# Chunk 1's down projection by Strassen's scheme over token halves, interleaved with two output projections

## The chip, the cores and the metric

One core of one Trainium2 chip runs the whole kernel. The metric is the device time of one execution in microseconds, lower is better. "Clock" is the mean granted TensorE clock as a share of full speed.

The engines are called as in the profile: PE is TensorE (matmuls), PEld its weight loads, DVE is VectorE, ACT is ScalarE, POOL is GpSimd, SP issues DMAs.

## The reference, cut to what matters

```python
# x: 1 x 2048 x 1024, w_down: 3584 x 1024, all bfloat16
x = A_x
h = x + attention(layernorm(x), A_wqkv) @ A_wo        # windowed attention, 32 heads
n = layernorm(h)
out = h + ((n @ B_w_gate) * (n @ B_w_up)) @ B_w_down  # no activation between
```

The kernel takes the tokens in four chunks of 512. For chunks 2 and 3 together ("pair stage" and "last stage") it already uses Strassen's scheme, that is seven products in place of eight, for the gate, up and down projections. Chunks 0 and 1 are plain.

## The kernel before: the parts that the change touches

```python
def ffn2(c, hf, hT, hs, between={}):                  # half of the output columns
    acc = [psum.tile([128, 512], F32, tag="mm", ...) for t in range(4)]
    for b in range(4):
        for j in range(7):
            f = b * 7 + j
            for t in range(4):
                nc.tensor.matmul(acc[t][:], lhsT=hT[f][:, bass.ts(t, 128)],
                                 rhs=wts["wd", c, hf, b][:, j, :],
                                 start=(f == 0), stop=(f == NF - 1))
            ...
    for t in range(4):
        ffn2_store(c, t, hf, acc[t], hs)              # DVE adds, SP stores
# ...
hT = ffn1(1, lnT2)                                    # first projection of chunk 1
scale_gu.rows(); scale_d.rows()
bg.finish(atts[2])
l2, hs2 = wo_ln2(2)                                   # output projection 2, layer norm
scale_gu.total(); scale_d.total()
# ... loads chunk 3's rows
ffn2(1, 0, hT, hs)                                    # down projection of chunk 1, half a
bg.finish(atts[3])                                    # ends with POOL issuing the oT load
l3, hs3 = wo_ln2(3)                                   # output projection 3, layer norm
activation_sums(l2, l3)
# ...
ffn2(1, 1, hT, hs, {0: first_sums})                   # half b
# ... pair stage, then the last stage:
conv_down(down["b12"])
scale_h.rows()
add_homes(t1v, Fv("b12"), Fv("b11"), ALU.subtract)
conv_down(down["b21"])                                # on DVE
```

`bg` is a helper that puts the attention of a chunk on DVE piece by piece between other work. In the traces each engine runs its instructions in the order of the program text: in the changed kernel POOL goes from the oT issue (483.05 us) to four conversions (486.77 to 514.74) and then to two subtractions (525.21 and 534.18).

## Time and profile before

| | before |
|---|---|
| time, median of 4 | 785.36 us (784.77 to 785.96) |
| PE busy | 774.1 us of 785.8 |
| first projection of chunk 1 ends | 449.5 us |
| output projections 2, 3 and down projection 1 | 449.5 to 525.9 |
| pair stage | 525.9 to 695.1 |
| last stage | 695.1 to 785.8 |

PE is the bound nearly everywhere. The lines that show it stand in the prediction below. One more row matters: the clock, part 2 of the page, in tenths of full speed for 40 slices of 20 us. It never leaves 9; a digit is the mean of its slice, so the 3.4 us of half clock near the start (0.57 from 9.3 to 12.7 us), which the prediction names, do not show in it.

```profile
PEclk9999999999999999999999999999999999999999
```

### The profile page before, as it was taken

Reading aid. Unit: us, or ns where it says so; the run is one execution under the profiler, and the core shown is the slowest. Engines: PE = TensorE matmul, PEld = TensorE weight load, DVE = VectorE, ACT = ScalarE, POOL = GpSimd, SP = SyncE. Lnnn points to the kernel's source line nnn. Section 1 sums busy time; section 2 is a strip of 40 time slices with the busy share of each in tenths; the row PEclk is TensorE's granted clock in tenths of the full one; section 3 lists DMA queues with packets and bytes.
Section 4 is the critical chain, followed back from the end, with each engine's and each line's share of the span. In section 5 each row is a group of like instructions: output and inputs, shape, how many; then the busy total and the mean of one; then the engine's idle time right before and its main releaser. Section 6 shows DMA issues by size and latency. Waiting matters only on the chain.

```text
span 785.8 us, 10287 instructions
## 1 busy us (share of the span) xinstructions
PE 774.1 (99%) x3670; PEld 359.2 (46%) x3732; DVE 583.6 (74%) x727; ACT 402.9 (51%) x919; POOL 150.9 (19%) x160
## 2 busy tenths in 40 slices
PE   8999999999999999999999999999999999999998
PEld 6544444444444444444444444444444444444444
DVE  5619999999899998999979971733443444579862
ACT  3626534323476652965656610116677777749240
POOL 0000000010000200002000020058678687600000
PEclk9999999999999999999999999999999999999999
DMA  7999594895965878867556489433332423730001
GB/s 248 269 197 243 150 286 98 244 311 127 337 203 170 260 243 234 277 197 264 198 161 208 139 202 328 101 100 102 107 90 72 108 62 100 257 118 28 1 27 54
DMA packets 183683, 135.94 MB, mean 173 GB/s; under 512 B 79056, under 2 KB 176464, under 8 KB 181584
## 3 DMA queue, kind: packets, MB, share of 16 engines
q1 hardware_dynamic: 180048, 113.27, 51.0%
q0 software_dynamic: 3584, 22.02, 8.1%
q8 instruction: 29, 0.48, 0.3%
q14 instruction: 22, 0.18, 0.1%
HBM read 106.95 MB, written 22.02 MB: 164 GB/s over the span
## 4 chain that ended last, share of the span: by engine, by line
PE 74%; DVE 20%; issue 2%; SPq 1%; DMA 1%; ACT 0%; DVEq 0%
PE pu L386 12%; PE acc L605 12%; PE pg L386 12%; PE pz L658 6%; PE py L658 6%; PE px L658 6%; PE wo L507 5%; DVE prod L426 4%; PE ps L386 3%; PE pv L658 3%; PE dx L837 3%; PE dy L837 3%; DVE pv L469 2%; DVE prod L428 2%; SPq L223 1%
## 5 line engine op out<-in xcount | busy, mean ns | idle before, releaser
L386 PE MATMUL ps<-lnT,w_qkv 128*128 128x512 bf16 x721 | 159.0, 379 | 0.8
L386 PEld LDWEIGHTS <-w_qkv 128*128 128x128 bf16 x736 | 71.9, 98 | 86.0 <-issue 0.3
L386 PE MATMUL pu<-lnT,w_wu 128*128 128x512 bf16 x438 | 105.1, 379 | 0.6
L386 PE MATMUL pg<-lnT,w_wg 128*128 128x512 bf16 x440 | 105.1, 379 | 0.4
L605 PE MATMUL acc<-w_wd,gs 128*128 128x512 bf16 x438 | 96.7, 379 | 0.5
L300 ACT CAST sg<-ps 128x512 bf16<-128x512 f32 x96 | 54.8, 590 | 52.7 <-PE ps L386 48.9
L469 DVE TENSOR_TENSOR pv<-vD,at 128x4096 bf16<-128x4096 bf16 x32 | 72.5, 2286 | 0.3
L426 DVE TENSOR_TENSOR prod<-qD,kD 128x4096 bf16<-128x4096 bf16 x32 | 72.4, 2284 | 0.1
L658 PEld LDWEIGHTS <-sw 128*128 128x128 f16 x448 | 43.8, 98 | 52.9
L386 PEld LDWEIGHTS <-w_wg 128*128 128x128 bf16 x448 | 43.8, 98 | 52.8
L605 PEld LDWEIGHTS <-gs 128*128 128x128 bf16 x448 | 43.8, 98 | 52.9
L386 PEld LDWEIGHTS <-w_wu 128*128 128x128 bf16 x448 | 43.8, 98 | 52.9
L179 ACT ACTIVATE rs<-mv,eps 128x1 f32<-128x1 f32 x32 | 9.5, 297 | 101.2 <-DVE mv L176 98.2
L585 ACT CAST us<-pu 128x512 bf16<-128x512 f32 x56 | 33.1, 591 | 50.4 <-PE pu L386 49.3
L507 PE MATMUL wo<-w_wo,oT 128*128 128x512 bf16 x251 | 55.6, 379 | 0.3
L658 PE MATMUL px<-lnT,ws 128*128 128x512 bf16 x211 | 52.6, 379 | 0.6
L658 PEld LDWEIGHTS <-ws 128*128 128x128 f16 x336 | 32.9, 98 | 39.6
L481 POOL DMA_DIRECT2D od<-oD x4 | 2.2, 544 | 249.3 <-DVE oD L479 162.5
L637 POOL TENSOR_TENSOR sw<-ws 128x512 f16<-128x512 f16 x28 | 32.3, 1154 | 87.8 <-PE acc L605 47.2
L580 ACT CAST gs<-pg 128x512 bf16<-128x512 f32 x56 | 33.1, 591 | 12.8 <-PE pg L386 8.7
L507 PEld LDWEIGHTS <-oT 128*128 128x128 bf16 x256 | 25.0, 98 | 30.2
L428 DVE TENSOR_TENSOR prod<-prod 128x4096 bf16<-128x4096 bf16 x16 | 36.6, 2288 | 0.3
(244 smaller groups left out, 1196.6 us busy)
## 6 DMA issues: line engine op xcount, KB each, us to landing
w_wg<-in_B_w_gate_dram SPq DMA_DIRECT2D x14, 1024.0 KB, 6.7
w_wu<-in_B_w_up_dram SPq DMA_DIRECT2D x14, 1024.0 KB, 5.6
w_wd<-in_B_w_down_dram SPq DMA_DIRECT2D x16, 896.0 KB, 8.1
w_wo<-in_A_wo_dram SPq DMA_DIRECT2D x8, 1024.0 KB, 7.4
w_pair<-in_B_w_gate_dram SPq DMA_DIRECT2D x14, 512.0 KB, 4.0
w_pair<-in_B_w_up_dram SPq DMA_DIRECT2D x14, 512.0 KB, 5.3
w_qkv<-in_A_wqkv_dram SPq DMA_DIRECT2D x5, 1024.0 KB, 9.7
kd<-sg SPq DMA_DIRECT2D x32, 144.0 KB, 2.8
```

Of the source, the lines that this page charges most:

```text
L300: nc.scalar.copy(sg[:, HB:HB + TC], ps[:])
L386: nc.tensor.matmul(ps[:], lhsT=wt[:, ko, bass.ts(j, 128)], rhs=rhs[:, ko, :], start=(ko == 0), stop=(ko == KO - 1))
L426: nc.vector.tensor_tensor(prod[:, j], qD[:], kD[:, :, o:o + SUB], ALU.mult)
L428: nc.vector.tensor_tensor(prod[:, :, 0:16], prod[:, :, 0:16], prod[:, :, 16:32], ALU.add)
L469: nc.vector.tensor_tensor(pv[:, j], vD[:, :, o:o + SUB], at[:, w, None, :].to_broadcast((128, DH, SUB)), ALU.mult)
L507: nc.tensor.matmul(ps[:], lhsT=oTs[c][:, kk, t, :], rhs=wts["wo", c, hf][:, kk, :], start=(kk == 0), stop=(kk == KO - 1))
L580: nc.scalar.copy(gs[:], pg[:])
L585: nc.scalar.copy(us[:], pu[:])
L605: nc.tensor.matmul(acc[t][:], lhsT=hT[f][:, bass.ts(t, 128)], rhs=wts["wd", c, hf, b][:, j, :], start=(f == 0), stop=(f == NF - 1))
L637: nc.gpsimd.tensor_tensor(sw[:, i, 0], a21, a22, ALU.add)
L658: nc.tensor.matmul(ps[:], lhsT=lhs[:, ko, :], rhs=rhs[:, ko, :], start=(fresh and ko == 0), stop=(ko == 3), skip_group_check=not fresh)
L837: nc.tensor.matmul(ps[:, bass.ds(lo, n)], lhsT=lhs[k][:, bass.ts(q, 128)], rhs=rhs[k][:, bass.ds(lo, n)], start=(fresh and k == 0), stop=( ...
```

## The change

Its intent: save 28 of 224 matmuls in chunk 1's down projection. Seven products P1 to P7 over token halves (2 row tiles each), contraction halves (14 blocks each) and output halves replace eight. The weights have to be converted from bf16 to scaled f16 and then combined (T1, T2, T3 and so on), and the activations likewise (S1, S2, S3). b11 to b22 are the quarters of the weights: the first digit is the half of the contraction, the second the half of the output columns. Each quarter lies in two tiles of 128x3584; `kx` and `vx` hold the two halves of T1 and later of P6's operand (T2 is written over b11), and `prodx`, `ox` and `lx` are the names that the profile gives to other tiles of b12 and b22. This preparation is spread over DVE, ACT and POOL, and the products are interleaved with output projections 2 and 3 so that there is time for it. The core of the diff, other lines cut:

```diff
-    hT = ffn1(1, lnT2)
-    l2, hs2 = wo_ln2(2)
-    ffn2(1, 0, hT, hs)
-    l3, hs3 = wo_ln2(3)
-    ffn2(1, 1, hT, hs, {0: first_sums})
+    def first_blocks():
+        ...
+        conv_down(dn["11"], nc.gpsimd)                      # POOL, 2 x 128x3584
+    hT = ffn1(1, lnT2, {0: scale_d.rows, 2: scale_d.total, 6: first_blocks})
+    conv_down(dn["21"], nc.scalar)
+    bg.finish(atts[2])
+    for q in range(2):
+        dprod(ex[q], q, E1["11"], fcells(dn["11"]), True)   # P1
+    def second_blocks():
+        bg.finish(atts[3])                                  # POOL: oT load of chunk 3
+        ...
+        conv_down(dn["12"] + dn["22"], nc.gpsimd)           # POOL, 4 x 128x3584
+    wo_adds(2, {1: scales, 3: second_blocks, 4: ..., 6: lambda: t1_half(0), 7: lambda: t1_half(1)})
+    for k in range(NP):
+        nc.vector.tensor_tensor(S1[k], EF["21"][k], EF["22"][k], ALU.add)
+    sub(dn["12"], dn["22"], dn["12"], nc.gpsimd)            # POOL, 2 x 128x3584
+    ...                                                     # P2, P3
+    wo_adds(3, {0: lambda: s2(0, 7), ..., 2: lambda: t2_half(0), ...})
+    for k in range(NP):
+        nc.gpsimd.tensor_tensor(EF["12"][k], EF["12"][k], EF["11"][k], ALU.subtract)
+    sub([dn["kx"], dn["vx"]], dn["21"], dn["11"])
+    for t in (2, 3):
+        ln_stats(2, t)
+    for t in range(4):
+        ln_stats(3, t)
+        ln_rows(2, t, l2)
+    for q in range(2):
+        dprod(ey[q], q, EF["11"], fcells(dn["11"]), False)  # P4
+        nc.scalar.copy(ex[q][:], ey[q][:])
+    ...                                                     # P5, P6, P7
-    for i in range(11):                                     # warm-up matmuls
+    for i in range(13):
-    conv_down(down["b21"])                                  # last stage
+    conv_down(down["b21"], nc.gpsimd)
```

## The prediction

> **What bounds the kernel now.** I read the page first (busy shares, chain that ended last, costliest groups), then the table of windows over the stretch that the change touches, then the timeline there. The page:
>
> ```profile
> PE 774.1 (99%) x3670; PEld 359.2 (46%) x3732; DVE 583.6 (74%) x727; ACT 402.9 (51%) x919; POOL 150.9 (19%) x160
> ...
> L605 PE MATMUL acc<-w_wd,gs 128*128 128x512 bf16 x438 | 96.7, 379 | 0.5
> ...
> L637 POOL TENSOR_TENSOR sw<-ws 128x512 f16<-128x512 f16 x28 | 32.3, 1154 | 87.8 <-PE acc L605 47.2
> ```
>
> TensorE is busy 774 of 786 us, and the down projections of chunks 0 and 1 (the second row) found it idle for 0.5 us in all: there is nothing to gain but matmuls, and any new wait is paid in full. The windows are: first projection of chunk 1 (353 to 449), then output projection 2, down projection 1a, output projection 3, down projection 1b (449 to 526):
>
> ```profile
> 353.00:449.00 96.00, 95.53 (x437) 43.55 (x445) 89.56 (x83) 60.94 (x110) 4.63 (x6) 1.00 0.58 189
> 449.00:526.00 77.00, 76.63 (x352) 34.90 (x357) 40.03 (x75) 5.62 (x19) 13.13 (x13) 1.00 0.70 190
> ```
>
> Columns after the width: busy PE, PE loads, DVE, ACT, POOL, then the granted clock. In the second window PE is full, DVE has 37 us free, ACT 71, POOL 64. So there is room for the new work; the question is its order. The timeline gives the order, and the row that I lean on most is the POOL one:
>
> ```profile
> 449.52 13.98 PE L507 MATMUL wo<-w_wo,oT 128*128 128x512 bf16 x63
> ...
> 463.80 3.71 POOL L484 DMA_DIRECT2D oT<-od  x4 [9.97 <-PE l1psgu L544]
> ```
>
> The transpose of chunk 3's attention into oT is issued by POOL, which stood idle for 10 us until output projection 2 had ended (463.5): there is one oT buffer, and those matmuls read it. The issue takes POOL 3.7 us. Before, nothing stood behind it.
>
> [...] The trace shows half clock only at the start (0.57 from 9.3 to 12.7 us), after idle; the rest says nothing. [...]
>
> **The change, part by part.**
>
> *Removed.* Down projection 1 is 2 x 4 x 28 = 224 matmuls of 128x512. Seven products over half the tokens (2 row tiles) and half the contraction (14 blocks) are 7 x 2 x 14 = 196. A matmul starts every 0.216 us (output projection 2: 64 in 13.98 us of the row above), so 28 x 0.216 = **6.05 us** go. One weight load of output projection fewer is off the path. In the last stage one conversion (2 x 1.15 us) leaves DVE; PE waited there 1.0 and 0.3 us on DVE's dn_t2 halves, so about **1 us** goes.
>
> *Added to PE.* One matmul for the new scale (0.2 us). Two more warm-up matmuls lie where PE waits for the first data anyway: 0.
>
> *Added elsewhere, hidden.* In the first projection ACT gets 28 absolute sums (0.62 + 0.19 us), 0.8 of each 3.46 us group; it was idle 1.1 us there, so it fits. POOL converts two blocks there, having 91 us free.
>
> *Added on the path.* PE's new order is P1 (28 matmuls, 6.05 us), output projection 2, P2, P3, output projection 3, P4, P5, P6, P7. By the order of instructions on each engine and what each waits for, two products come too early for their operands.
>
> P3 multiplies S1 by T1 = b12 - b11. POOL converts b12, in two blocks, but behind the issue of oT for chunk 3. With E the end of output projection 2: issue ends E+0.3+3.7 = E+4.0; [...]then DVE, in its queue: the second half of T1 (1.95, the 128x3584 subtraction is 2.01 in the last stage), the 14 additions for S1 (14 x 0.20; half of the 0.41 of a 512 addition) 2.8, and the result of P2 that frees the accumulator 0.75: E+15.7. PE has only P2 until then, E+6.1. **Wait: 9.6 us.**
>
> P5 starts from a copy of P4's accumulator on ACT, and that copy stands behind chunk 2's normalised rows, which need DVE. With G the end of output projection 3, DVE does: last addition 0.7, two subtractions 3.9, six layer-norm statistics of 1.44 each (two of 0.68 less overlap, plus 0.21 and gaps: 492.20 to 493.64 in the timeline) 8.6, four small ones 0.6: G+13.8. Then ACT, one row of 128x1024 (1.06) and the copy (0.57), with handovers 2: G+15.8. PE has P4, until G+6.3. **Wait: 9.5 us**, and DVE comes to G about 1.7 us late, as in that stretch it is given S2, T2 and statistics beside the additions: **11.2 us.**
>
> [...]the clock should drop in each[...]: **about 4 us** for both. P6, P7 and the start of the pair products are then late enough that their operands are there.
>
> Sum: 785.4 - 6.05 - 1 + 0.2 + 9.6 + 11.2 + 4 = 803.4; I take **803 us**.
>
> **The rivals.**
>
> (a) *All hidden.* If conversions and statistics keep up, only the arithmetic remains: 785.4 - 6.05 - 1 + 0.2 = 778.5. For it: the free time in the window, and that such a schedule will have been tuned with a profile at hand, with warm-up counts and engines chosen finely. Against it: [...]the two queues above are in the program. Nothing can make the change faster by over 2%, since that is 15.7 us.
>
> (b) [...]POOL's two subtractions of 128x3584 (7 x 1.154 = 8 us each, estimate) and 14 small ones now lie beside DVE's two-input work. If each blocks the other, both waits grow by up to a subtraction: 810 to 825. [...]no row of the trace speaks for or against.
>
> (c) *One wait only.* If the conversions took 1 us, P3's wait would be 5.4; if the statistics of chunk 3 were done during output projection 3, P5's wait would be about 2. Either alone gives 790 to 796. At 8 us per conversion P3's wait would be 19 and the sum 813.
>
> (d) *Weight loads.* The blocks of 0.9 MB land in 8.1 us and are issued well ahead; the queue's share was 0.70. The loads for b12 and b22 wait for attention 3's buffers, which are free at 453. Hidden, I think; one landing late would add 1 to 3 us at P2 or P3.
>
> **Range and chances.** Each of the two waits rests on queue order[...] and on durations of which one (conversion on POOL) is not measured: plus or minus 6. The clock is plus or minus 3,[...] a better overlap than I see only downward. Low 789 (one wait halved and no clock loss), high 817[...]. Slower by over 2% begins at 801.1, just under the middle, and I give the tuner's eye some weight: slower 0.53, same 0.46, faster 0.01.
>
> **What would show it.** Right: an idle time of PE of 7 to 13 us ahead of P3, released by DVE's T1 or result, with POOL going straight from the oT issue into its conversions; a second of 8 to 14 us ahead of P5, released by ACT's copy, which itself follows the row activations; granted clock of half in the window after each; matmuls in the two down projections down by 28. Wrong: PE busy without a gap from 449 to the pair stage (then rival a, near 779);[...] DVE or POOL operations much longer where they lie side by side than alone (rival b).

## The result, and the profile after

The changed kernel takes 879.89 us (median of 4, 879.69 to 880.63). Ratios here are the mean time of one kernel's fast runs over that of the other's of the same rounds, so not quite the ratio of the medians: 1.1205, with a 95% interval of 1.1186 to 1.1225. The forecast was 803 with 817 as the upper end: the direction was right, the size was far off.

First the rows that answer to those shown before: part 1 of the page, the clock row, and the two windows with the same columns.

```profile
PE 780.9 (89%) x3707; PEld 356.4 (41%) x3707; DVE 677.3 (77%) x799; ACT 450.6 (51%) x1019; POOL 255.6 (29%) x184
...
PEclk9999999999999999999978755979999999998999
```

```profile
353.00:449.00 96.00, 95.64 (x444) 43.17 (x442) 89.54 (x80) 69.12 (x150) 26.43 (x7) 1.00 0.59 192
449.00:526.00 77.00, 29.03 (x114) 11.78 (x113) 56.81 (x46) 29.36 (x50) 44.28 (x11) 0.67 0.29 93
```

In the stretch from 449 to 526 us PE falls from 76.63 us to 29.03, and its clock to 0.67. The view of PE's waits says what it waited for (waiter, releaser: us in total, times, longest):

```profile
PE ex L782 <- DVE h L787: 55.5, 1, 55.5
PE ex L782 <- ACT ex L925: 13.9, 1, 13.9
PE ex L782 <- DVE gs L597: 8.6, 2, 6.8
PE dy L550 <- DVE rowbh L546: 7.2, 1, 7.2
PE wo L827 <- DVE h L829: 2.6, 2, 1.4
PE ex L782 <- POOL w_dn L763: 2.5, 1, 2.5
```

The 55.5 us are ahead of P3, the 13.9 ahead of P5: the two waits of the prediction. The 8.6 and 2.5 stand inside P1, the 7.2 in the last stage; those I had not foreseen. By stage, from the starts of PE's rows in the two timelines:

| stretch | before | after | difference |
|---|---|---|---|
| start to the end of chunk 1's first projection | 449.5 | 447.0 | -2.6 |
| output projections 2, 3 and down projection 1 | 76.4 | 163.4 | +87.0 |
| pair stage | 169.2 | 169.2 | 0 |
| last stage | 90.7 | 98.6 | +7.9 |

The profile before is of an execution of 787.53 us, 2.2 us over its median of 785.36; so the differences add up to 92.3 us and not to the 94.5 of the medians, and part of the -2.6 belongs to that one execution (see the warm-up matmuls below).

Now the timeline of POOL and of DVE around the long wait (start, us, engine, line, operation; in brackets the idle time before). E, the end of output projection 2, is 482.7 here.

```profile
483.05 3.70 POOL L490 DMA_DIRECT2D oT<-od  x4 [14.81 <-PE wo L827]
486.77 9.34 POOL L763 TENSOR_SCALAR w_dn<-w_dn,sbd 128x3584 f16<-128x3584 bf16 x1
496.11 9.32 POOL L763 TENSOR_SCALAR prodx<-prodx,sbd 128x3584 f16<-128x3584 bf16 x1
505.42 9.32 POOL L763 TENSOR_SCALAR ox<-ox,sbd 128x3584 f16<-128x3584 bf16 x1
514.74 9.32 POOL L763 TENSOR_SCALAR lx<-lx,sbd 128x3584 f16<-128x3584 bf16 x1
525.21 6.94 POOL L775 TENSOR_TENSOR w_dn<-ox,w_dn 128x3584 f16<-128x3584 f16 x1 [1.16 <-DVE kx L775]
534.18 7.06 POOL L775 TENSOR_TENSOR prodx<-lx,prodx 128x3584 f16<-128x3584 f16 x1 [2.02 <-DVE vx L775]
```

```profile
496.15 28.91 DVE L775 TENSOR_TENSOR kx<-w_dn,w_dn 128x3584 f16<-128x3584 f16 x1 [13.92 <-POOL w_dn L763]
...
525.59 8.45 DVE L775 TENSOR_TENSOR vx<-prodx,w_dn 128x3584 f16<-128x3584 f16 x1
533.96 9.65 DVE L884 TENSOR_TENSOR es<-gs,gs 128x256 f16<-128x256 f16 x14
```

Two things are to be seen. The queue is as predicted: POOL goes from the oT issue straight into the conversions. But one conversion takes 9.3 us, about three times what the prediction's chain leaves for it, and DVE's subtraction kx, which needs only the first converted block and starts at 496.15, is listed at 28.91 us and ends about 1 us after the last of three conversions on which it does not depend. It is the same operation that takes 2.0 us elsewhere: the same line later in the same trace gives 2017 ns. Likewise vx and S1 (es) are long exactly while POOL's two subtractions run. This looks like a DVE that is held, not one that works slower; the experiments test it.

### The profile page after: what moved, and what is told of

The parts are those of the page before. It is cut to its first block, busy times and chain, and to the rows that moved or that the text cites. A ratio compares the mean times of both kernels' runs of the same rounds, so it can differ in the third digit from the quotient of the medians.

```text
span 878.1 us, 10555 instructions
## 1 busy us (share of the span) xinstructions
PE 780.9 (89%) x3707; PEld 356.4 (41%) x3707; DVE 677.3 (77%) x799; ACT 450.6 (51%) x1019; POOL 255.6 (29%) x184
## 3 DMA queue, kind: packets, MB, share of 16 engines
q0 software_dynamic: 3584, 22.02, 7.2%
## 4 chain that ended last, share of the span: by engine, by line
PE 77%; DVE 16%; issue 4%; POOL 1%; DMA 1%; ACT 1%; SPq 0%; DVEq 0%
PE ps L392 18%; PE pu L392 8%; PE pg L392 8%; PE py L675 6%; PE px L675 6%; PE acc L624 6%; PE pz L675 6%; PE dx L782 5%; DVE pv L475 4%; PE ex L782 3%; PE wo L513 3%; PE pv L675 3%; PE dy L782 3%; PE wo L827 2%; DVE kx L775 1%
## 5 line engine op out<-in xcount | busy, mean ns | idle before, releaser
L475 DVE TENSOR_TENSOR pv<-vD,at 128x4096 bf16<-128x4096 bf16 x32 | 88.8, 2797 | 0.3
L675 PE MATMUL px<-lnT,ws 128*128 128x512 bf16 x224 | 55.2, 379 | 0.0
L782 PE MATMUL ex<-kx,es 128*128 128x512 f16 x14 | 4.8, 502 | 55.5 <-DVE h L787 55.5
L763 POOL TENSOR_SCALAR w_dn<-w_dn,sbd 128x3584 f16<-128x3584 bf16 x3 | 33.7, 11246 | 63.4 <-DMA h<-in_A_x_dram 63.4
L624 PE MATMUL acc<-w_wd,gs 128*128 128x512 bf16 x224 | 48.5, 379 | 0.0
L782 PE MATMUL ex<-w_dn,gs 128*128 128x512 f16 x70 | 21.7, 470 | 25.0 <-ACT ex L925 13.9
L775 DVE TENSOR_TENSOR kx<-w_dn,w_dn 128x3584 f16<-128x3584 f16 x2 | 30.9, 15464 | 13.9 <-POOL w_dn L763 13.9
```

The lines of the kernel that those rows point to most:

```text
L475: nc.vector.tensor_tensor(pv[:, j], vD[:, :, o:o + SUB], at[:, w, None, :].to_broadcast((128, DH, SUB)), ALU.mult)
L624: nc.tensor.matmul(acc[t][:], lhsT=hT[f][:, bass.ts(t, 128)], rhs=wts["wd", c, hf, b][:, j, :], start=(f == 0), stop=(f == NF - 1))
L675: nc.tensor.matmul(ps[:], lhsT=lhs[:, ko, :], rhs=rhs[:, ko, :], start=(fresh and ko == 0), stop=(ko == 3), skip_group_check=not fresh)
L763: eng.tensor_scalar(dst, src, sc, None, ALU.mult)
L775: eng.tensor_tensor(f16(d[:, 0:NH, :]), f16(a0[:, 0:NH, :]), f16(a1[:, 0:NH, :]), ALU.subtract)
L782: nc.tensor.matmul(ps[:, bass.ds(lo, n)], lhsT=lhs[k][:, bass.ts(q, 128)], rhs=rhs[k][:, bass.ds(lo, n)], start=(fresh and k == 0), stop=( ...
```

## The experiments

**Theory L:** a POOL elementwise instruction that reads SBUF shuts out DVE operations with two inputs from SBUF while it runs; that, and conversions three times as long as the estimate, make up what the prediction lacked. **Rival Q:** only the order of POOL's queue and its slow conversions count; the long DVE operations have another cause (operands, dependences). "Lock" and "held" are short names for what the rows show, a DVE operation listed long beside POOL's work; what in the chip makes it so is not shown.

### Conversions back on DVE, in three steps

Step one, b12 and b22; step two, also b11 in the first projection and b21 in the last stage; step three, also the two POOL subtractions of 128x3584 and the fourteen of 128x256.

```diff
-        conv_down(dn["12"] + dn["22"], nc.gpsimd)      # step one
+        conv_down(dn["12"] + dn["22"])
-        conv_down(dn["11"], nc.gpsimd)                 # step two
+        conv_down(dn["11"])
-    conv_down(down["b21"], nc.gpsimd)
+    conv_down(down["b21"])
-    sub(dn["12"], dn["22"], dn["12"], nc.gpsimd)       # step three
+    sub(dn["12"], dn["22"], dn["12"])
-        nc.gpsimd.tensor_tensor(EF["12"][k], EF["12"][k], EF["11"][k], ALU.subtract)
+        nc.vector.tensor_tensor(EF["12"][k], EF["12"][k], EF["11"][k], ALU.subtract)
```

> The changed kernel with one edit: the four conversions of b12 and b22 run on VectorE, not on GpSimd. Theory L (a GpSimd elementwise instruction locks VectorE's two-input SBUF operations out for its whole length, and several in a row are let through together): the subtraction of 28.9 us ahead of P3 goes back to about 2 us, PE's wait of 55.5 us ahead of P3 shrinks to 10 to 25 us (the two GpSimd subtractions of about 7 us still lie beside VectorE's work there), the time is 835 to 850. Rival Q (only the order of GpSimd's queue behind the oT issue and its slow conversions count, the long VectorE operation is something else[...]): the conversions leave the queue, but the subtraction stays far over 2 us; the wait is 30 us or more.

> The changed kernel with all eight GpSimd conversions on VectorE (b11 in the first projection, b12 and b22, and b21 of the last stage); the two GpSimd subtractions of 128x3584 and the 14 of 128x256 stay. Theory L: as with b12 and b22 alone, and also the two multiplications of 10.45 us in the first projection go back to 2.28, PE's waits of 11 us in P1 fall under 5, and the wait of 7.2 us in the last stage goes: 815 to 830. Rival Q: less than 10 us better than b12 and b22 alone, as those conversions stood ahead of nothing else in the queue.

> As the kernel with all conversions on VectorE, and the GpSimd subtractions (two of 128x3584, fourteen of 128x256) on VectorE too: no GpSimd elementwise work is left beside VectorE's before the pair stage. Theory L: VectorE has more to do (3.9 and 2.8 us) but is never locked out: S1, S2 and S3 take 2.8 us each, P3 waits under 8 us, the time is 798 to 812, which is where the prediction put its second wait plus the clock. Rival Q: moving 7 us of work onto the busier engine gains nothing or loses a few us.

Measured: 846.49, 826.49 and 813.57 us, against 785.69 for the kernel before. The times are within what theory L gave or, in step three, 1.6 us over it, though each step puts work onto the busier engine; P3's wait in step three was to be under 8 us and is 8.8. In step one P3's wait is 23.1 us. The conversions then take DVE 1.15 us each. In step two the two subtractions on POOL are still there, and DVE's vx and S1 stay at 8.53 and 9.67 us; in step three they are 2.01 and 2.90. PE's waits in step three:

```profile
PE ex L782 <- ACT ex L925: 13.8, 1, 13.8
PE ex L782 <- DVE h L787: 8.8, 1, 8.8
PE ex L782 <- DVE w_dn L763: 5.0, 1, 5.0
```

With POOL out of the way P3 waits 8.8 us and P5 13.8, where the prediction said 9.6 and 11.2, and the time is 10 us over the 803 predicted. For P5 the predicted chain is there. For P3 the likeness is luck, for the chain is another one: in this trace the conversions end on DVE at 472.5, before output projection 2 does (474.4), so POOL's oT issue (474.70 to 478.42) holds none of them up. DVE works without a gap from 467.53 to the result that frees P3 (489.8): on the conversions, T1, S1 and the two subtractions taken over from POOL.

### The last stage alone

```diff
-    conv_down(down["b21"], nc.gpsimd)
+    conv_down(down["b21"])
```

> The changed kernel with the last stage's two conversions of b21 back on VectorE, as in the kernel before. Theory L: the four multiplications listed at 9.62 us go back to 1.4, PE's wait of 7.2 us for the row of sums goes, and the time falls by 6 to 8 us less the 2.3 us of VectorE work that may show: 872 to 876. Rival: the conversion only stood in a queue of its own, nothing changes, 879 to 881.

Measured: 871.86 us, 8.0 less. In the changed kernel DVE's four small multiplications stood beside the second conversion:

```profile
780.42 9.62 DVE L714 TENSOR_TENSOR kx<-kx,up 128x512 bf16<-128x512 bf16 x4
...
781.07 9.57 POOL L763 TENSOR_SCALAR dn_b21b<-dn_b21b,sbd 128x3584 f16<-128x3584 bf16 x1
```

It is the +7.9 us of the last stage. The prediction had put -1 there.

### The lock by itself, in the kernel before

Nothing depends on these POOL operations; they work on a spare buffer beside chunk 3's attention. The first run has conversions, the second one conversion and nine memsets, the third one long and six shorter independent conversions.

```diff
+                if c == 1 and len(hT) == 16:
+                    scr = lnTp.tile([128, KO, TC], BF, tag="lnT", name="scr")[:, 0:7, :]
+                    s = tick()                              # a DVE memset, to place it in time
+                    nc.gpsimd.tensor_scalar(scr, lnT[:, 0:7, :], s, None, ALU.mult)
+                    for i in range(3):                      # first run
+                        nc.gpsimd.tensor_scalar(scr.bitcast(F16), scr, s, None, ALU.mult)
+                    for i in range(9):                      # second run
+                        nc.gpsimd.memset(scr, 1.0)
```

> The kernel before, with four conversions of 128x3584 of a spare buffer on GpSimd, back to back, while VectorE does chunk 3's attention in the first projection of chunk 1, and four more kinds of one-input operation on GpSimd in the quiet part of the down projection; nothing depends on any of them. Theory L: one VectorE operation of the attention or more is listed at 9 to 38 us in place of 2.28, and the time grows by 20 to 37 us though no result is used. Rival (the long VectorE times come from data dependences or from operands of the changed kernel): VectorE's times stay at 2.28 and the time stays within 2 us. In the quiet part all four kinds take about 9.3 us if the rate is that of any one-input operation on GpSimd, and fewer for copies or an immediate factor if it is the scalar operand or the type that makes it slow.

> The same place in the kernel before, but one conversion and nine memsets of 128x3584 of the spare buffer. If only a GpSimd operation that reads SBUF shuts VectorE's two-input operations out, VectorE's times are 2.28 beside the memsets and one operation is 9 to 11 us beside the conversion; the time grows by about 7 to 10 us at most. [...]

> The kernel before with GpSimd work of no use beside chunk 3's attention: one conversion of 128x3584, then six of 128x1536 (4 us each by the 9.3 for 3584) of which neighbours do not depend on each other, so that the next can start at once. With dependent conversions VectorE got in after each one (10.5 us listed, four times). If VectorE is let in only where GpSimd makes a pause for a dependence: one VectorE operation of about 25 us. If it is let in after each instruction in any case: six of about 5 us. Also a plain cast of 128x3584 where VectorE is quiet: 3.2 us, as at the end of the first such run.

Measured: 816.50, 797.95 and 809.80 us against 785.34 (785.77 in the third's call). Timelines of the first run, POOL and then DVE's operations over 2.4 us, and of the second run, again POOL and then DVE:

```profile
411.70 10.52 POOL L604 TENSOR_SCALAR scr<-lnT,tick 128x3584 bf16<-128x3584 bf16 x1 [48.44 <-issue]
422.31 31.82 POOL L606 TENSOR_SCALAR scr<-scr,tick 128x3584 f16<-128x3584 bf16 x3
```

```profile
413.01 10.48 DVE L469 TENSOR_TENSOR pv<-vD,at 128x4096 bf16<-128x4096 bf16 x1
423.75 10.46 DVE L469 TENSOR_TENSOR pv<-vD,at 128x4096 bf16<-128x4096 bf16 x1
434.25 10.43 DVE L474 TENSOR_TENSOR oD<-pv 128x4096 bf16<-128x4096 bf16 x1
444.94 10.46 DVE L469 TENSOR_TENSOR pv<-vD,at 128x4096 bf16<-128x4096 bf16 x1
```

```profile
423.39 28.23 POOL L606 MEMSET scr<- 128x3584 bf16 x9
```

```profile
414.12 10.48 DVE L469 TENSOR_TENSOR pv<-vD,at 128x4096 bf16<-128x4096 bf16 x1
...
424.86 2.28 DVE L469 TENSOR_TENSOR pv<-vD,at 128x4096 bf16<-128x4096 bf16 x1
```

Four conversions hold four attention operations 8.2 us each; beside nine memsets in a row the same operations take their 2.28 us. So here POOL's conversions, which read SBUF, held these two-input operations, its memsets, which only write, did not, and no dependence is needed: for them theory L is shown, and rival Q's other cause is not needed. The two engines took turns: a conversion with its held operation took 10.6 us (31.82 for three), 1 us less than the 9.33 and 2.28 one after the other.

Theory L is too narrow, though. The multiplication that normalises a row (`ln`, 128x1024, one tensor and two per-partition factors from SBUF) takes 0.55 us in the kernel before. In these three runs one of them each is held as well: it is listed at 4.51 us and ends 0.28 us after a conversion, at 2.19 us and ends 0.29 us after a cast, and, in the second run, at 5.18 us, ending 0.28 us after a memset put later in that run (468.36 to 471.46). Its own listed start (466.56) lies before that memset's, so that the memset held it is the likely reading and not shown. In the fourth attempt below another multiplication of this kind (`ws`, 128x4096, one tensor and one per-partition factor) is listed at 1.97 us beside POOL's `sw` work (from 527.13), and at 1.29 with none beside it (514.33). The held `ln` also explains why the second run's time grew by 12.6 us, more than the 7 to 10 expected: PE waited 9.0 us there for DVE's additions, 5.4 of them for the one behind this operation, and after it the clock was 0.50 from 472.4 to 478, which costs it some 2.8 us.

The quiet part of the first run gives POOL's rates where DVE has little to do: 9.33 us for the multiplication by a per-partition factor, with bf16 or f16 out, 9.26 with an immediate factor, and 3.24 us for a plain cast. It is the multiplication that is slow, not the type.

```profile
498.43 9.33 POOL L619 TENSOR_SCALAR scr<-scr,tick 128x3584 f16<-128x3584 bf16 x1 [6.57 <-DVE tick L575]
507.86 9.33 POOL L620 TENSOR_SCALAR scr<-scr,tick 128x3584 bf16<-128x3584 bf16 x1
517.28 9.26 POOL L621 TENSOR_SCALAR scr<-scr 128x3584 f16<-128x3584 bf16 x1
526.61 3.24 POOL L622 CAST scr<-scr 128x3584 f16<-128x3584 bf16 x1
```

In the third run the six shorter conversions (4.0 us each) made six DVE operations of 5.28 us: DVE got in after each instruction. My guess that it is let in only at a dependence is refuted. Why kx was held for three conversions in a row in the changed kernel stays open. It came again where the same program part was run again (28.92 us in the run with b21 alone), and twice in other forms: in the run with casts below (11.19 us, three casts) and in the split run (23.18 us). In all four the DVE operation was listed 0.04 to 0.11 us after a POOL instruction, but so was one in the changed kernel's pair stage (596.22, 0.06 us after) that was held for one POOL instruction only; so that alone does not decide it.

### Conversions cut into pieces

```diff
-            to_f16(f16(t[:, 0:NH, :]), t[:, 0:NH, :], scale_d.s, eng)
+            for k in range(NH):                             # on POOL only
+                to_f16(f16(t[:, k, :]), t[:, k, :], scale_d.s, eng)
```

> The changed kernel with each GpSimd conversion of 128x3584 cut into seven of 128x512, back to back, still on GpSimd. If the lock goes to the other engine at each end of an instruction (theory L with alternation): VectorE's long subtraction shrinks from 28.9 to 4 us or less and the multiplications from 10.45 to about 4; but the 14 small additions then wait for a piece of 1.3 us each: 850 to 870. If a row of GpSimd instructions keeps the lock as long as there is a next one (theory L, no alternation): the same 28.9 us and 875 to 885.

Measured: 866.76 us. The two turn about: the attention operations beside the pieces take 2.66 to 2.69 us, kx 2.51. P3's wait fell to 27.4 us, but the 128x3584 subtractions of POOL stayed whole, and one now met T2's second half (23.18 us), which made PE wait 19.2 us ahead of P4. So the cut helps where it is made; the gain was eaten where it was not made.

### How much is length, how much is the lock

```diff
-            eng.tensor_scalar(dst, src, sc, None, ALU.mult)
+            eng.tensor_copy(dst, src)                       # on POOL only
```

> The changed kernel with each GpSimd conversion done as a plain cast, without the factor (the result is wrong on purpose). In a run before, a cast of 128x3584 took GpSimd 3.24 us where the multiplication took 9.3[...]. Theory: the cast locks VectorE as well, only for a shorter time. Then PE's wait ahead of P3 falls from 55.5 to about 31 us (four casts of 3.2 after the oT issue, then as before 20 us of VectorE work beside the two GpSimd subtractions), the waits in P1 under 4, the one in the last stage under 1: about 838 us, 830 to 846. Rival A (a cast does not lock): P3's wait is 15 to 20 and the time 820 to 828. Rival B (the length of the conversions does not matter): 870 or more.

Measured: 835.38 us, P3's wait 31.6 us, kx 11.19 us. Conversions as plain casts (3.17 to 3.18 us each for b12 and b22), about the length that the prediction's chain leaves for one, take away 44.5 of the 94.5 us; with the lock still in place the time is 32 us over the prediction. That is the theory's forecast (838 us, wait about 31), and neither rival's. (The result was still correct, against what I had written.)

### Warm-up matmuls

```diff
-    for i in range(11):
+    for i in range(13):
```

> The kernel before with 13 warm-up matmuls in place of 11, nothing else. The first output projection starts 2.8 us earlier in the changed kernel's trace. If the two warm-up matmuls do that (the clock does not fall to half between 9.3 and 12.7 us), the time is 782 to 783.5 and that window's clock is 1.0. If it is chance in the landing of the first loads, the time stays at 785.0 to 785.8.

Measured: 785.74 us, ratio 1.0003 (0.9986 to 1.0019): no effect. In its profile the clock from 9.2 to 12.6 us was 1.0, but this is not the work of the two matmuls: in four other profiles with 11 of them (the three lock runs above and the last run below) it is 1.0 there as well (the five executions of the last one list 1.0 over the whole span, the one profiled as "before" 0.997). The half clock belongs to the one execution that was profiled as "before". Of the 2.6 us by which the changed kernel's profile is ahead at the start, 1.2 are that execution's own: in the last run below, also with 11, the first projection of chunk 1 ends at 448.3 and not 449.5. For the rest no cause is shown; the landing of the first loads differs between profiles (PE waited 2.1 us for them before, 0.4 after).

### P4's copies ahead in the queue

In the kernel of step three, one block is moved:

```diff
     load_pair(1)
+    for q in range(2):
+        dprod(ey[q], q, EF["11"], fcells(dn["11"]), False)
+        nc.scalar.copy(ex[q][:], ey[q][:])
     for t in (2, 3):
         ln_stats(2, t)
     for t in range(4):
         ln_stats(3, t)
         ln_rows(2, t, l2)
-    for q in range(2):
-        dprod(ey[q], q, EF["11"], fcells(dn["11"]), False)
-        nc.scalar.copy(ex[q][:], ey[q][:])
```

> The kernel with no GpSimd elementwise work in the chunk 1 part, and one block moved in the program: the matmuls of P4 with the copies of its accumulator on ScalarE now stand ahead of the layer-norm statistics and rows, so that the copy is not queued behind them. TensorE's order is the same. Theory (second step of the prediction: P5 waits only for the queue of ScalarE and VectorE): PE's wait of 13.8 us ahead of P5 goes; about 5 us of it come back ahead of the first pair product, whose operands now are late; with the clock that does not drop, 801 to 806 us against 813.6. Rival (the work on VectorE is too much, the wait only moves): the wait comes back whole ahead of the pair products, 811 to 816.

Measured: 811.00 us. The 13.8 us ahead of P5 are gone, so the queue was their cause, but 9.1 us came back ahead of P6, whose accumulator is freed by a DVE result that now stood behind the statistics. Only 2.6 us of time were gained. The time is that of the rival, though it placed the wait ahead of the pair products: taking the queue away is not enough, because DVE has the work to do in any case.

### A version with order and lock put right

Five attempts, each mending what the one before showed. The first moves all POOL elementwise work to DVE and ACT and spreads the preparation; its essence:

```diff
-    conv_down(dn["11"], nc.gpsimd)
+    # on DVE, inside the first projection: after block 5 and in block 6
-    wo_adds(2, {1: scales, 3: second_blocks, 4: a22, 5: a22, 6: t1_half(0), 7: t1_half(1)})
+    second_blocks()                     # loads only
+    wo_adds(2, {0: conv b12a on DVE, 1: scales, conv b12b on DVE and b22 on ACT,
+                2: t1_half(0), 3: t1_half(1), 4: a22, 5: a22, 6: ln_stats(2, 0), 7: ln_stats(2, 1)})
-    wo_adds(3, {0: s2, 1: s2, 2: t2_half(0), 3: t2_half(1), 4: ln_stats(2, 0), 5: ln_stats(2, 1)})
+    s2(0, 14); t2_half(0); t2_half(1)
+    wo_adds(3, {0: ln_stats(2, 2), 1: ln_stats(2, 3), 2: rows of chunk 2 and T3, 3: T3,
+                4: ln_stats(3, 0), 5: ln_stats(3, 1)})
+    # P4 with its copies, then the other statistics and chunk 3's rows
-    conv_down(down["b21"], nc.gpsimd)
+    conv_down(down["b21"], nc.scalar)
```

> All of it put right: no GpSimd elementwise work in the chunk 1 part; b11 converted on VectorE inside the first projection, b12 and T1 in the idle time of VectorE at the start of output projection 2, b22 and b21 on ScalarE, S2, S3 and T2 ahead of output projection 3, chunk 2's statistics spread over both output projections, the copies of P4 ahead of chunk 3's rows. If queues and the lock were all that the change lacked: no wait of PE over 3 us between the first projection and the pair stage, clock near 1.0, and 778 to 783 us, so up to 1% under the kernel before. If VectorE's sum of work does not fit: 784 to 795.

Measured: 794.20 us, with waits of 6.0 us (P3) and 3.5 us (P6): the second of the two cases. The second attempt loads b12's second half earlier and puts the two subtractions for P6 on POOL, beside DVE's statistics:

```diff
+    dn["raw"] = lnTp.tile(...)          # loaded in the first projection
+    to_f16(f16(dn["12"][1][:, 0:NH, :]), dn["raw"][:, 0:NH, :], scale_d.s)
-    sub([dn["kx"], dn["vx"]], dn["21"], dn["11"])
+    sub([dn["kx"], dn["vx"]], dn["21"], dn["11"], nc.gpsimd)
```

> The reordered kernel again, with its two waits of 6.0 and 3.5 us attacked: b12's second block is loaded early into a free buffer, so that VectorE no longer sits 4.7 us on its load; statistics of chunk 2 only after P2; and the two subtractions for P6 on GpSimd (7 us each), placed beside VectorE's additions from PSUM and statistics, which are no two-input operations from SBUF. If those are not locked out, VectorE's 0.68 us for such an addition and 1.27 for two statistics stay as they are, and the time is 779 to 785. If they are, they are listed at several us and the time is 788 to 800.

Measured: 792.94 us, a time of the range given for additions and statistics that are locked out. But they were not: what was held was something else. Timeline of DVE, and POOL's subtraction beside it:

```profile
494.39 1.28 DVE L181 BATCH_NORM_STATS2 st<-h 128x6 f32<-128x512 bf16 x2
495.71 0.21 DVE L182 BATCH_NORM_AGGREGATE mv<-st 128x2 f32<-128x12 f32 x1
495.83 6.05 DVE L848 SCALAR_TENSOR_TENSOR nb<-mv,rs 128x1 f32<-128x1 f32 x4
501.81 0.68 DVE L835 TENSOR_TENSOR h<-wo,h 128x512 bf16<-128x512 f32 x1
```

```profile
494.70 6.96 POOL L777 TENSOR_TENSOR vx<-w_dn,w_dn 128x3584 f16<-128x3584 f16 x1
```

This is the clearest picture of the lock: beside a POOL subtraction two statistics take their usual 1.28 us, while four operations on one element per partition, with two inputs from SBUF, take 6.05 us (three of them take 0.24 us at 509.81, with no POOL work beside them). Additions from PSUM beside the other subtraction (486.15 to 494.74) took their usual 0.64 to 0.68. That subtraction is itself listed at 8.59 us in place of 6.96: it started beside a DVE subtraction of two SBUF inputs (485.89 to 487.91), so here the holding went the other way too (8.60 us again in the fourth attempt, started at 487.58 beside a DVE subtraction from 487.33). In these traces the size of the DVE operation does not decide, its kind does. The third attempt puts these small products on ACT and splits T2; the fourth and fifth mend the order once more:

```diff
-        nc.vector.scalar_tensor_tensor(nbs[c][:, t:t + 1], mv4[:, t, 0:1], -1.0, rs4[:, t:t + 1], ...)
+        nc.scalar.activation(nbs[c][:, t:t + 1], mv4[:, t, 0:1], ACTF.Copy, scale=rs4[:, t:t + 1])
+        nc.scalar.activation(nbs[c][:, t:t + 1], nbs[c][:, t:t + 1], ACTF.Copy, scale=-1.0)
     # third: T2's halves in different groups of output projection 3, POOL's subtractions after the second
     # fourth: both halves in one group, ahead of POOL's; pair weights loaded in group 3
     # fifth: P4's copies ahead of chunk 2's last row
```

> The second reordered kernel with one thing mended: there four VectorE operations on single elements (two operands from SBUF) stood 6 us behind a GpSimd subtraction and held the copy ahead of P5 back (wait 6.1 us), while 1.27 us statistics and 0.64 us additions from PSUM ran at full speed beside the same subtraction. These small products now run on ScalarE, and part of T3 and T2 moves into output projection 3. Theory: the wait of 6.1 us and most of the 1.9 us ahead of it go and the clock stays at 1.0; 782 to 786, which is no more than the kernel before, as VectorE is then full from 454 to 520 us. If 779 or less, the change has its arithmetic gain at last. If 788 or more, another wait has come up.

> The third reordered kernel with its own slip mended: GpSimd's first subtraction for P6 started between the two halves of T2 and held the second half 6.5 us (8.49 listed for 2.0), which held PE 5.0 us; now both halves stand together ahead of it, the pair weights are loaded earlier, and the results of P5 and the last sums stand ahead of the wait for those weights. If that is all: waits of PE in this part under 3 us in sum, 783 to 786, level with the kernel before within 0.2%. If VectorE has simply too much work there: 788 or more, with waits spread over P5 to the pair products.

> The last reordered kernel (784.05 us) with its one wait over 2 us attacked in the way that the experiment with the copies showed: the copies of P4 stand on ScalarE ahead of chunk 2's last row and chunk 3's first statistics. If the wait ahead of P5 (2.2 us) and the half clock after it go: 780.5 to 782.5, 0.4 to 0.6% under the kernel before. If it comes back at P6 or at the pair products: 783.5 to 785.

Measured: 793.88, 784.05 and 784.52 us. The third made a new wait by its own slip: POOL's first subtraction started between the halves of T2 and held the second for 6.5 us (8.49 listed for 2.01). The fourth is 0.9983 of the kernel before (0.9971 to 0.9996), the fifth 0.9989 (0.9976 to 1.0003). In the fifth the 2.2 us ahead of P5 are gone and 3.7 us are there at the pair products instead. DVE is busy for 70.9 of 77 us from 449 to 526 in the fourth, against 40.0 in the kernel before. That DVE's sum of work holds the rest of the gain is the likely reading, since a wait taken away came back elsewhere both times that P4's copies were moved; no run with less work on DVE shows it.

One part of these versions by itself, in the kernel before:

```diff
-    conv_down(down["b21"])
+    conv_down(down["b21"], nc.scalar)
```

> The kernel before with one small part of the change done in another way: the conversion of b21 in the last stage on ScalarE, not on VectorE (before) or GpSimd (changed). PE's waits of 1.0 and 0.3 us for dn_t2 should go: 784.0 to 784.8 against 785.4 to 785.8, about 0.15%.

Measured: 784.62 us, ratio 0.9990 (0.9976 to 1.0004): about what was expected, but not clear of zero. So of the 1.4 us of the fourth version up to half may be this line and not the scheme.

## Why the prediction was right or wrong

- **The gain.** 28 matmuls fewer at 0.216 us: not contradicted. The fourth version is 1.4 us faster (its middle stretch takes 74.4 us in place of 76.4), with 3.3 us of new waits in PE's list (2.2 and 1.1) and the clock at 0.98 in that stretch.
- **The failed step: P3's wait of 9.6 us, measured 55.5. Its first wrong term is the time of a conversion on POOL, an estimate that no row backs.** Measured: 9.3 us. The estimate is near what a plain cast took (3.24 us); the multiplication took about three times that. This was the one duration without a row in the trace, and the text said so, but its upper case of 8 us led only to 813 because of the next step.
- **The second wrong term: the lock, named as rival (b) and mis-sized.** "Both waits grow by up to a subtraction" looked only at POOL's subtractions beside DVE. It left out that the conversions themselves hold DVE. The chain ahead of P3 was to have, after b12's conversions, 1.95 + 2.8 + 0.75 us of DVE work. Measured from the end of b12's second conversion (505.4) to P3 (544.3): 38.9 us. Two more conversions of 9.3 us are in it and both POOL subtractions (6.94 and 7.06 us). That POOL goes straight from the oT issue into the conversions was right; the issue was never moved by itself, so its share of some 4 us is not tested. With plain casts in that place (3.17 to 3.18 us) the wait is still 31.6 us, three times the forecast, with kx listed at 11.19, vx at 8.45 and S1 at 9.65 us beside POOL's work.
- **"POOL converts two blocks there, having 91 us free".** Free time on POOL was not free here, for its use held DVE: DVE was 93% busy in the first projection (89.56 of 96 us), two multiplications of the attention took 10.45 us in place of 2.28, and P1 had waits of 11.1 us, which with the conversions on DVE are 5.0.
- **"About 1 us goes" in the last stage.** It became +7.9 us, by the same lock.
- **P5's wait.** 11.2 predicted, 13.9 measured and 2.6 ahead of it in output projection 3. Its mechanism was right: it goes when the copies are moved. DVE came to the end of output projection 3 some 4.6 us late, not 1.7, in the changed kernel because S2 was held by POOL's fourteen small subtractions (3.39 and 4.83 us for two halves that take 1.49 elsewhere). In step three, where nothing holds S2, DVE comes to the end of output projection 3 1.7 us late, as predicted.
- **The clock.** 4 us predicted, an estimate; the one row of half clock in the trace before was the 3.4 us at the start. The waits were more and longer: the slow stretches of P1, P3 and P5 add up to about 9 us (for example P3's 28 matmuls took 8.82 us in place of 6.05, and the clock from 544.3 to 550.3 was 0.53). That it halves after each of the two gaps was right (0.50 from 544.3 to 548.5 us and from 590.1 to 593.5).
- **Right:** ACT's absolute sums fit into the first projection (PE lost nothing there, 95.64 us busy of 96), the weight loads were hidden (the only load in PE's list of waits is w_qkv, 0.4 us), the pair stage took the same 169.2 us.
- **The sum:** waits 11.1 + 55.5 + 2.6 + 13.9 = 83.1, less 6.05, plus about 9.9 left for the clock, is the +87.0 us of the middle stretch (the new scale's matmul stands in it, but the older scale's has moved out of it); +7.9 at the end and -2.6 at the start make 92.3, the difference of the two profiled spans.
- **Slips in the prediction's own sums.** Its low end is called "one wait halved and no clock loss", but 803.4 - 4.8 - 4 is 794.6; 789 is about one wait gone whole. In (c), conversions of 1 us give 803.4 - 4.2 = 799.2, which lies outside the 790 to 796 stated. Neither bears on the miss.

## What to carry to other kernels

Before moving work to an engine that has time to spare, ask what it does there to the engine that has none: here GpSimd work that read SBUF held VectorE's two-input operations for nearly its whole length (28.91 us listed for 2.0 beside three conversions of 9.3), and taking eight conversions off the idle engine again was worth 53 us, nine times what the 28 matmuls save. Where a duration that the argument rests on has no row in the trace, give it the range of its neighbours (the two-input row was 1154 ns for 512 elements, which makes about 8 us for 3584), and measure it alone first. A scheme that saves the bound engine 0.8% pays only if its preparation fits the next engine; here VectorE went from 40 to 71 us of 77, and what could be kept was 0.17%, of which up to half may be the conversion of b21.
